# Gated attention mix: scaled V copies on VectorE, gate logits in one bank, paced loads, a last round in halves, and another order of semaphore waits

## The chip, the cores and the metric

One core of one Trainium2 chip. The time is the device time of one execution in microseconds (us), the median of several executions; the profile is of one of them, and its span is about 2 us shorter than the time. The engines are PE (TensorE matmuls; PEld is its weight loads), ACT (ScalarE), DVE (VectorE), POOL (GpSimd) and SP (the engine that issues most DMAs). The granted clock is the TensorE clock that the throttle allowed, as a share of full speed.

## The reference

```python
x = A_x                                          # (1, 2048, 512), bf16
g = sigmoid((x * gate_w).sum(-1, keepdims=True))
# A: softmax attention, 32 heads of 16
a = softmax(q @ k.T * 16 ** -0.5) @ v @ wo_A      # per head, 2048 x 2048 scores
# B: linear attention with phi(t) = where(t > 0, t + 1, exp(t)) + 1e-6
b = (phi(q) @ (phi(k).T @ v)) / (phi(q) @ phi(k).sum()) @ wo_B
out = g * a + (1 - g) * b
```

The time goes into A: 32 x 2048 x 2048 scores must be exponentiated. The kernel cuts them into rounds, each of 64 units of 128 x 512 scores.

## The kernel before

A scheduler written in Python walks through a model of the machine, decides the order of instructions on each engine, and then issues that order with semaphore waits. ACT does most of the exponentials, two units per instruction:

```python
return C(AC, 500, 427 * n + 49, lambda: nc.scalar.activation(
    P[:, slot, 0:512 * n], bank(b0, n), ACT.Exp, scale=ESC), ...)
```

The other units are evicted by VectorE as integers Z (a bit-pattern exponential), and shifted copies of Z, by VectorE or GpSimd, give further terms. Each term is multiplied on PE with a differently scaled copy of V. That is why V is scaled after its own eviction, here on GpSimd:

```python
for k in range(1, NTERM):
    yield po(690, lambda k=k: nc.gpsimd.tensor_scalar(Vc[:, k, vs]..., Vc[:, 0, vs]..., COEF[k], 1.0,
                                                      op0=ALU.mult, op1=ALU.mult), [r_V[vs]], [r_V[vs]])
```

An instruction names the semaphores that it must wait for in the order in which its operands are listed. Each becomes a wait ahead of the instruction:

```python
def add(self, fn, deps=(), inc=True, dma_sem=None):
    waits = []
    for d in deps:
        ...                                     # sem, val of the dependency
        for k, (s2, v2) in enumerate(waits):
            if s2 is sem:
                if val > v2:
                    waits[k] = (sem, val)
                break
        else:
            waits.append((sem, val))
...
for waits, fn, inc, dma_sem in E.ops:
    for sem, val in waits:
        eng.wait_ge(sem, val)
    h = fn()
```

The gate logits are computed in four PSUM banks, one per 512 rows of x, and everything behind them is engine work: a VectorE transpose per bank, a GpSimd copy, one exponential on ACT, a reciprocal, four reordering copies on VectorE. The weights of B (and those of A's later head groups) are loaded with one DMA each of 1.5 MB:

```python
def t_wb():
    yield ("DMA", wB[:], B_wqkv.rearrange("(cc p) n -> p cc n", p=128), semWB, 16, 12000.0, [], [r_wB], False, True)
```

The softmax here doesn't subtract the row's maximum and nothing guards it: scores larger than these inputs give would overflow.

## Time and profile before

| | before |
|---|---|
| time, median of 3 (range) | 681.13 (680.4 to 681.41) us |
| span of the profiled run | 679.8 us |
| first exponential starts | 10.67 us |
| exponentials of two units | 695, steady step 0.917 us |
| ACT time lost between first and last | 8.03 us: 6.61 up to 40 us, 0.11 from 40 to 80, 1.31 later |
| last exponential ends, tail behind it | 671.53, 8.30 us |

"ACT time lost" is worked out from the trace. For each pair of neighbouring ACT instructions between the first and the last exponential I take the step from end to end and subtract the undisturbed step: 0.917 us for an exponential of two units, 0.478 for one of the linear attention, 0.25 for the gate's.

Two views of before, to be held against the kernel after. The first is the chain of work that ended last, by engine; the second is what PE's weight loads waited for (us in total, times, longest):

```profile
ACT 42%; PE 42%; issue 14%; DVE 1%; DMA 1%; ACTq 0%; POOL 0%; POOLq 0%
```

```profile
PEld ps L363 <- ACT P L756: 239.9, 601, 0.8
PEld ps L363 <- issue: 116.0, 492, 0.8
...
PEld ps L363 <- DVE Z L672: 13.0, 52, 0.4
```

In the names, ps are the PSUM banks, Qz and KT what the score matmuls read, P ACT's exponentials, Z VectorE's, Vc the scaled copies of V. PE waits for ACT 601 times: the score matmuls of the next units may start only when an exponential has freed its banks. ACT sets the pace and PE follows it.

### The profile page before, as it was taken

How to read it: one execution, taken by the hardware profiler on the slowest of the kernel's cores; microseconds unless marked ns; L12 is line 12 of the kernel's file. 1: busy time of each engine (PE TensorE's matmuls, PEld its weight loads, DVE VectorE, ACT ScalarE, POOL GpSimd, SP SyncE). 2: the span in 40 equal slices, each digit the busy share in tenths (PEclk: the TensorE clock that was granted, in tenths of full speed). 3: DMA queues.
4: the chain of work that ended last, by engine and by line, in shares of the span. 5: the costliest groups of instructions: out<-in, count | busy, mean ns of one | idle time of the engine just before them, and what ended most of it. 6: DMA issues, size and time to landing. Idle time of an engine off the chain costs nothing.

```text
span 679.8 us, 24140 instructions
## 1 busy us (share of the span) xinstructions
PE 664.7 (98%) x9886; PEld 203.6 (30%) x9910; DVE 605.1 (89%) x1073; ACT 658.2 (97%) x734; POOL 550.7 (81%) x626
## 2 busy tenths in 40 slices
PE   8899999999999999999999999999999999999997
PEld 3323232322222222322333322222233322222222
DVE  5789889989899998989899998898999998998995
ACT  5799999999999999999999999999999999999995
POOL 4669878898888888888878888878589888889883
PEclk9999999999999999999999999999999999999999
DMA  6500002100000000000000100000003220000000
GB/s 132 203 18 3 9 2 72 33 2 10 2 9 2 7 6 2 10 2 2 12 3 23 52 10 1 10 3 2 1 11 53 38 49 25 17 18 17 18 18 32
DMA packets 27869, 15.96 MB, mean 23 GB/s; under 512 B 19697, under 2 KB 26737, under 8 KB 27761
## 3 DMA queue, kind: packets, MB, share of 16 engines
q1 hardware_dynamic: 26416, 13.91, 8.0%
q8 instruction: 79, 1.29, 0.8%
q10 hardware_dynamic: 1344, 0.52, 0.3%
q14 instruction: 30, 0.24, 0.1%
HBM read 6.69 MB, written 2.10 MB: 13 GB/s over the span
## 4 chain that ended last, share of the span: by engine, by line
ACT 42%; PE 42%; issue 14%; DVE 1%; DMA 1%; ACTq 0%; POOL 0%; POOLq 0%
ACT P L756 41%; PE ps L363 32%; PE ps L369 9%; ACT eb L1029 1%; DMA xnat<-wA 1%; DVE Z L672 0%; PE ps L884 0%; ACTq L1433 0%; DVE wA L1135 0%; DVE Z L734 0%; DVE T L994 0%; ACT KT L906 0%; ACT wA L1174 0%; POOL warm L407 0%; ACT gt L980 0%
## 5 line engine op out<-in xcount | busy, mean ns | idle before, releaser
L756 ACT ACTIVATE P<-ps 128x1024 bf16<-128x1024 f32 x695 | 645.3, 1126 | 7.4 <-PE ps L363 7.4
L724 POOL TENSOR_TENSOR Z<-Z,mcon 128x512 int32<-128x512 int32 x464 | 477.7, 1054 | 77.6 <-DVE Z L672 46.1
L672 DVE TENSOR_SCALAR Z<-ps 128x512 int16<-128x512 f32 x658 | 441.9, 683 | 57.0 <-PE ps L363 49.8
L363 PE MATMUL ps<-Z,Vc 128*17 128x512 bf16 x1974 | 283.8, 383 | 0.2
L363 PE MATMUL ps<-Qz,KT 32*128 32x512 bf16 x2048 | 272.1, 385 | 4.0 <-ACT P L756 2.3
L363 PE MATMUL ps<-P,Vc 128*17 128x512 bf16 x1390 | 253.0, 383 | 0.0
L363 PEld LDWEIGHTS ps<-Qz,KT 32*128 32x128 bf16 x2048 | 67.9, 91 | 260.4 <-ACT P L756 237.8
L363 PEld LDWEIGHTS ps<-Z,Vc 128*17 128x17 bf16 x1974 | 64.4, 88 | 78.2 <-issue 50.7
L734 DVE TENSOR_SCALAR Z<-Z 128x1024 int16<-128x1024 int16 x194 | 79.8, 430 | 0.2
L363 PEld LDWEIGHTS ps<-P,Vc 128*17 128x17 bf16 x1390 | 57.5, 88 | 55.1 <-issue 42.9
L363 PE MATMUL ps<-warm 128*32 128x512 bf16 (+13 forms) x618 | 59.3, 330 | 4.5 <-issue 3.0
L369 PE MATMUL ps<-xT,wA 128*32 128x512 bf16 x512 | 42.9, 382 | 0.0
L1030 POOL TENSOR_SCALAR eb<-eb 128x512 f32<-128x512 f32 x32 | 19.9, 622 | 16.9 <-DVE Z L734 7.4
L961 POOL TENSOR_SCALAR Vc<-Vc 128x576 bf16<-128x576 bf16 x32 | 21.9, 685 | 8.0 <-DVE Vc L958 5.2
L1017 POOL TENSOR_TENSOR T<-T,rg 128x256 bf16<-128x256 f32 x31 | 19.6, 634 | 8.6 <-DVE Z L734 5.3
L363 PEld LDWEIGHTS ps<-warm 128*32 128x32 bf16 (+1 forms) x642 | 20.8, 95 | 17.5 <-issue 10.3
L994 DVE STREAM_TRANSPOSE T<-ps 128x512 f32<-128x512 f32 x32 | 22.7, 709 | 3.0 <-PE ps L363 2.9
L369 PE MATMUL ps<-wA,xT 128*32 128x128 bf16 x1024 | 22.1, 220 | 2.2 <-issue 2.2
L369 PE MATMUL ps<-wB,xT 128*32 128x512 bf16 x256 | 23.4, 382 | 0.0
L369 PE MATMUL ps<-wA,OAT 128*32 128x512 bf16 x256 | 23.0, 381 | 0.0
L369 PE MATMUL ps<-xT,wB 128*32 128x512 bf16 x256 | 22.4, 383 | 0.0
L369 PE MATMUL ps<-wA,xnat 128*32 128x512 bf16 x256 | 22.3, 381 | 0.0
(79 smaller groups left out, 283.4 us busy)
## 6 DMA issues: line engine op xcount, KB each, us to landing
Qz<-QT SPq DMA_DIRECT2D x120, 16.0 KB, 1.8
wA<-in_A_wqkv_dram SPq DMA_DIRECT2D x1, 1536.0 KB, 7.8
wB<-in_B_wqkv_dram SPq DMA_DIRECT2D x1, 1536.0 KB, 11.9
xnat<-in_A_x_dram SPq DMA_DIRECT2D x3, 512.0 KB, 5.3
out_dram<-outt SPq DMA_DIRECT2D x12, 128.0 KB, 1.7
wA<-in_A_wo_dram SPq DMA_DIRECT2D x1, 512.0 KB, 4.3
wA<-in_B_wo_dram SPq DMA_DIRECT2D x1, 512.0 KB, 5.2
out_dram<-wA SPq DMA_DIRECT2D x4, 128.0 KB, 1.8
```

The source lines that it names most:

```text
L363: return lambda: nc.tensor.matmul(o, lhsT=l, rhs=r, start=start, stop=stop, skip_group_check=sg)
L369: h = nc.tensor.matmul(o[32 * j:32 * j + 32], lhsT=l[:, 32 * j:32 * j + 32], rhs=r, start=start, stop=stop, skip_group_check=True)
L672: return C(DV, 400, 533 * n + 74, lambda: nc.vector.tensor_scalar(o, i, ZB, 0.0, op0=ALU.add, op1=ALU.max), [r_bank[b] for b in bks], r_Z[ ...
L724: return C(PO, 400, 70 + 484 * n, lambda: nc.gpsimd.tensor_tensor(Z[:, z, 0:512 * n].bitcast(I32), Z[:, z0, 0:512 * n].bitcast(I32), mcon[ ...
L734: return C(DV, 450 if hot else 300, 69 + 134 * n, lambda: nc.vector.tensor_scalar(Z[:, z, 0:512 * n], Z[:, z0, 0:512 * n], float(m), None, ...
L756: return C(AC, 500, 427 * n + 49, lambda: nc.scalar.activation(P[:, slot, 0:512 * n], bank(b0, n), ACT.Exp, scale=ESC), [r_bank[b0 + k] fo ...
L961: yield po(690, lambda k=k: nc.gpsimd.tensor_scalar(Vc[:, k, vs].rearrange("p a b c -> p (a b c)"), Vc[:, 0, vs].rearrange("p a b c -> p ( ...
L994: yield dv(607, lambda: nc.vector.transpose(T1[:, a, :], bank(7)), [r_bank[7]], [r_T1[a]])
L1017: yield po(640, lambda: nc.gpsimd.tensor_tensor(t2[:, :, 16 * par:16 * par + 16], t1[:, :, 0:16], rg[:, a, :].unsqueeze(2).to_broadcast([1 ...
L1029: yield ac(480, lambda: nc.scalar.activation(eb[:, i, :], bank(b), ACT.Exp), [r_bank[b]], [r_eb[i]])
L1030: yield po(640, lambda: nc.gpsimd.tensor_scalar(eb[:, i, :], eb[:, i, :], 1.0 + 1e-6, 0.0, op0=ALU.min, op1=ALU.max), [r_eb[i]], [r_eb[i]])
```

## The change

It was meant to relieve GpSimd (the V copies go to VectorE), to shorten the gate's chain (one bank, 16 columns instead of 64 for the exponential, small SBUF-to-SBUF DMAs in place of transposes and copies), to stop large loads from holding all DMA engines (pieces of 384 KB, released over time), to start sooner (the first K only to half), to shorten the end (the last round in halves), and to let an instruction name last the semaphore that is expected last. Some constants of the scheduler were tuned again with it, so the order of instructions differs all over.

```diff
@@ waits of an instruction
-        for d in deps:
-            if d is None:
-                continue
+        for d in sorted([d for d in deps if d is not None], key=lambda d: d.fin if isinstance(d, _Ev) else 0.0):
...
                 if s2 is sem:
-                    if val > v2:
-                        waits[k] = (sem, val)
+                    val = max(val, v2)
+                    del waits[k]
                     break
-            else:
-                waits.append((sem, val))
+            waits.append((sem, val))
@@ scaled copies of V
-                yield po(690, lambda k=k: nc.gpsimd.tensor_scalar(Vc[:, k, vs]..., Vc[:, 0, vs]..., COEF[k], 1.0,
-                                                                  op0=ALU.mult, op1=ALU.mult), [r_V[vs]], [r_V[vs]])
+                yield ("OP", DV, 214, lambda k=k: nc.vector.tensor_scalar(Vc[:, k, vs]..., Vc[:, 0, vs]..., COEF[k], None,
+                                                                  op0=ALU.mult), [r_V[vs]], [r_V[vs]], None, 1.0, True)
@@ gate (both cut)
-            for qc in range(NQC):
-                b = yield ("BANK",)
-                ... matmuls with 128 columns, dv transpose of the bank, po copy to ge ...
-            yield ac(300, ... gt <- exp(-ge) ...)
-            ... po + 1, dv reciprocal, po 1 - g, four dv copies to gnat ...
+            b = yield ("BANK",)
+            ... matmuls of all four chunks, 32 rows each, one dv transpose ...
+            yield ac(230, ... ge[:, 0, :] <- exp(-gl) ...)
+            ... po + 1, dv reciprocal ...
             for qc in range(NQC):
+                for a in range(4):
+                    yield ("DMA", gt[32 * a:32 * (a + 1), qc, :], ge[32 * qc:32 * (qc + 1), 0, :], semGN, 256, 2500.0, ...)
+            ... po 1 - g, four DMAs to gnat ...
@@ loads
-        add_task(t_wb(), 0.9, 1, "WB")
+        for cc in range(NCC):
+            add_task(t_load(cc, NCC, wA[:, cc, :], wsrc[:, cc, :], semWA, 3500.0, ..., "wa"), 0.3 + 0.15 * cc, 0.9, f"WA{cc}")
+            add_task(t_load(cc, NCC, wB[:, cc, :], wsrcB[:, cc, :], semWB, 3500.0, ..., "wb"), 0.9 + 0.2 * cc, 1.8, f"WB{cc}")
@@ not shown: first K in halves, pairs of rounds sharing one reciprocal, last round in halves, 18 Z buffers for 16, scheduler constants
```

## The prediction

> **What bounds the kernel now.** I read the page's busy table first, then ACT's timeline over the whole span, then the groups, then the stages in windows.
>
> ```profile
> PE 664.7 (98%) x9886; PEld 203.6 (30%) x9910; DVE 605.1 (89%) x1073; ACT 658.2 (97%) x734; POOL 550.7 (81%) x626
> ...
> L756 ACT ACTIVATE P<-ps 128x1024 bf16<-128x1024 f32 x695 | 645.3, 1126 | 7.4 <-PE ps L363 7.4
> L724 POOL TENSOR_TENSOR Z<-Z,mcon 128x512 int32<-128x512 int32 x464 | 477.7, 1054 | 77.6 <-DVE Z L672 46.1
> L672 DVE TENSOR_SCALAR Z<-ps 128x512 int16<-128x512 f32 x658 | 441.9, 683 | 57.0 <-PE ps L363 49.8
> ...
> L734 DVE TENSOR_SCALAR Z<-Z 128x1024 int16<-128x1024 int16 x194 | 79.8, 430 | 0.2
> ...
> L961 POOL TENSOR_SCALAR Vc<-Vc 128x576 bf16<-128x576 bf16 x32 | 21.9, 685 | 8.0 <-DVE Vc L958 5.2
> ```
>
> PE shows 98% and ACT 97%. PE's share contains warm-up matmuls on a dummy tile that the program puts into free slots, so it cannot name the bound. ACT has no filler: 695 exponentials of two score units each. The other 658 units (695 x 2 + 658 = 2048) are done by VectorE and GpSimd with integer additions. In the 700-odd ACT instructions only 7.4 us of waiting stand before an exponential. From the records' ends I worked out the step from one exponential to the next: 651 of 660 neighbours are within 10 ns of 0.92 us. The longest unbroken run gives 0.917 (158.86 us for 173, less 0.2 us by which the last outlasts its step). So ACT is saturated from 36 us to 671 us, and the time is: start of the first exponential + 695 x 0.917 + 32 other exponentials of about 0.48 us each (start to the next start in the timeline) + ACT's idle + the tail behind the last exponential.
>
> Where ACT is not busy is in its timeline:
>
> ```profile
> 9.58 0.59 ACT L906 CAST KT<-ps 128x512 bf16<-128x512 f32 x1 [1.86 <-PE ps L369]
> 10.67 9.27 ACT L756 ACTIVATE P<-ps 128x1024 bf16<-128x1024 f32 x10 [0.50 <-PE ps L363]
> 21.18 8.36 ACT L756 ACTIVATE P<-ps 128x1024 bf16<-128x1024 f32 x9 [1.24 <-PE ps L363]
> 32.74 1.02 ACT L756 ACTIVATE P<-ps 128x1024 bf16<-128x1024 f32 x1 [3.21 <-PE ps L363]
> 35.62 28.52 ACT L756 ACTIVATE P<-ps 128x1024 bf16<-128x1024 f32 x31 [1.85 <-PE ps L363]
> ...
> 542.17 129.36 ACT L756 ACTIVATE P<-ps 128x1024 bf16<-128x1024 f32 x141 [0.36 <-PE ps L363]
> 675.67 1.23 ACT L1174 CAST wA<-ps 128x512 bf16<-128x512 f32 x2 [4.15 <-PE ps L369]
> ```
>
> The first exponential starts at 10.67 us. Then 1.24 us are lost at 20 us and 3.21 + 1.85 = 5.06 us around 30 to 36 us; later only 0.19 + 0.36. The last exponential ends at 671.53, 8.3 us before the span's end. The 5.06 us have their cause in these windows and in PE's timeline:
>
> ```profile
> 26.00:28.00 2.00, 2.00 (x60) 0.85 (x48) 2.00 (x4) 2.00 (x3) 1.92 (x3) 1.00 1.03 416
> 28.00:30.00 2.00, 0.71 (x30) 0.45 (x29) 0.83 (x2) 1.53 (x2) 1.28 (x2) 1.00 0.58 219
> 30.00:32.00 2.00, 1.11 (x10) 0.33 (x13) 0.77 (x2) 0.00 (x0) 0.00 (x0) 0.70 0.03 12
> 32.00:34.00 2.00, 2.00 (x23) 0.42 (x19) 0.97 (x3) 1.02 (x1) 1.83 (x3) 0.50 0.04 8
> ...
> 30.89 0.30 PE L369 MATMUL ps<-wA,xT 128*32 128x128 bf16 x4 [2.18 <-issue]
> ...
> wB<-in_B_wqkv_dram SPq DMA_DIRECT2D x1, 1536.0 KB, 11.9
> ```
>
> (Columns: stretch, length, busy PE, PEld, DVE, ACT, POOL, granted clock, DMA share, GB/s.) Two loads of 1.5 MB, issued at 19 and 19.5 us, hold all DMA engines from 22 to 29 us. At 28.7 us PE stops for 2.18 us in the middle of a group of equal matmuls, waiting for no engine ("issue"). The page counts 1.29 MB on an instruction queue of the same engines, and its packets of 16 KB come at 21.1 and only again at 28.5 us, just behind the loads. I read the gap as PE out of instructions. Afterwards the granted clock is 0.50 from 31 to 34 us, which stretches the loss.
>
> **What the Trainium skill says.** "Perfetto Trace Analysis", section Identifying the Most-Contended Engine: occupancy names the bound for Scalar and Vector, matmul busy time does not for Tensor. The trace agrees: PE's 98% contains fillers. "ScalarE: Activation LUTs", section What ACT_TABLE_LOAD costs: an ACTIVATE with a pointer bias takes about 280 ns + 0.833 per element, neighbours overlapping by about 93 ns. For 1024 columns that is 1133; the trace has 1126, but a step of 917, an overlap of 0.21 us; I use the measured step. "Runtime: NRT & Kernel Launch", section Instruction fetch mechanics: instructions come in blocks of 16 KiB over a DMA queue of the sequencer's own, mostly hidden. The trace shows such packets, and one that does not look hidden. "SBUF — State Buffer", section Who interferes with whom: a VectorE instruction in a two-port mode and a GpSimd instruction exclude each other. The scaled copies of V, moved to VectorE, would be such instructions; the program orders them against GpSimd with semaphores, as it does the 194 integer shifts.
>
> **The change part by part**, with counts from the order of instructions in the two programs.
>
> *Exponentials.* 693 instead of 695: 2 x 0.917 = -1.8 us. The gate's exponential shrinks from 128x64 (0.41 us) to 128x16: about -0.2.
>
> *V copies.* 32 of 0.685 leave GpSimd (-21.9 us); 32 come to VectorE. The 1024-column shift takes 0.43 and costs 79.8/194 = 0.41 of throughput; for 576 columns I estimate 0.26, so +8.3 us. Nine more shifts (+3.9) and four more evictions of scores (+2.7) come; pairing the reciprocals, four gate transposes fewer and no gate reordering on VectorE take away about 6.5. VectorE ends near 613, GpSimd near 520. Neither is on the path while ACT is saturated, so directly this is worth nothing.
>
> *The 1.24 us at 20 us.* Ten exponentials have run then and there are ten P buffers; the eleventh starts 0.45 us after the first P x V matmuls (20.73), which come behind V's scaled copies (GpSimd, 17.70 to 19.23). With copies of about 0.26 on VectorE the first P x V wave stands before one more score group than before, and starts with six P matmuls where it had two. I take -0.9 and leave 0.3.
>
> *Paced loads.* Each 1.5 MB load becomes four of 384 KB, released over about half a round, a round being about 20 us (655/32). At 416 GB/s a piece takes an estimated 0.95 us; between pieces instruction packets can pass. The 5.06 us go, I leave 0.3: -4.8.
>
> *K in halves.* Ahead of the first scores stand 16 matmuls of 256 columns in place of 16 of 512: the 32 before took 1.9 us, so 16 take 0.95 and halves save 0.45. The cast of K on ACT falls from 0.59 to about 0.37. Together -0.65 for the first exponential.
>
> *Last round in halves.* Before, from 672.53 to 674.95 one chain of five VectorE instructions (0.72, 0.26, 0.18, 0.43, 0.71), then casts to 676.91 and four output issues whose last lands at 679.34. Halves of about 0.40, 0.22, 0.17, 0.28, 0.40 with gaps of 0.03 make 1.6 us each: the first is done 0.8 us earlier, the second 0.8 later. The first two output tiles go out early, three of four casts on ACT, but the last issue still begins near 677.4 against 677.52 and takes the same 1.8 to land. So -0.2, not a microsecond.
>
> *Waits.* The reordered semaphore waits change when PE's sequencer gets to a matmul by fractions of 0.1 us; with ACT saturated and two score sets in turn, 0 on the path.
>
> Sum: -1.8 - 0.2 - 0.9 - 4.8 - 0.65 - 0.2 = -8.55, from 681.1: **672.5 us**, a ratio of 0.987.
>
> **The rivals.** (1) The gap at 30 us is not hunger for instructions but something that pacing does not move. For: one gap, once, and the packet landed (28.48 + 1.08) 1.3 us before PE went on. Against: it follows the only stretch with DMA share 1.0, on matmuls that wait for nothing. Then only about 3.8 us are gained: 677. (2) VectorE becomes the bound: the added 8 us plus port exclusion raise it from 89% to 91%, and score evictions come late, so the eviction banks stay full and PE delays score groups. For: the V copies cluster in the first rounds, where VectorE is already near 2.00 of 2.00 in some windows. Against: over the middle it has 5 to 10% free, and the offloaded units went up by four, not down. It would show as ACT idle of some microseconds at each V group: 676 to 680. (3) The saved GpSimd time lets the scheduler move more off ACT than counted. Against: the count is fixed, 693. (4) The tail gains more than I give, if the late casts overlap better: 671.5. (5) Smaller loads come too late for the second head group and idle ACT near 35 us: 674 to 676.
>
> **Range and chances.** The saturated middle is fixed by a count and a step and moves little; the head holds most of the uncertainty, more of it upwards. 8 in 10: 669 to 676.5. Faster by over 2% needs under 667.5, that is 5 us beyond a sum that already takes nearly all idle of the head: 0.07. Slower needs 694.8: 0.02. Within 2%: 0.91.
>
> **What would show it.** First exponential near 10.0; ACT idle between first and last exponential of about 1.2 us instead of 6.9; no PE "issue" gap over 1 us and a granted clock of 1.0 throughout 20 to 40 us; DMA share below 1.0 there; the step unchanged at 0.917 with 693 instructions; GpSimd busy near 520 and VectorE near 613; last exponential to end still about 8 us. I am wrong if ACT's step or its idle in the middle changed, if a gap remains at 30 us, or if the tail falls under 7 us.

## The result and the profile after

| | before | after |
|---|---|---|
| median (range) | 680.88 (680.4 to 681.41), 4 runs | 684.38 (683.45 to 685.51), 4 runs |
| span of the profiled run | 679.8 | 682.5 |
| first exponential | 10.67 | 9.88 |
| exponentials | 695 | 693 |
| ACT lost: up to 40, 40 to 80, later | 6.61, 0.11, 1.31 | 3.19, 4.29, 5.82 |
| tail | 8.30 | 8.31 |

The ratio is 1.0052, 95% interval 1.0035 to 1.0069. A ratio here is the mean time of one kernel's runs over the mean of the other's runs of the same rounds, so it is not quite the ratio of the medians. The kernel became slower by 3.5 us where 8.6 us less were predicted; 684.38 lies well outside the range of 669 to 676.5. All outputs are right.

The page of the kernel after: busy time by engine, the chain that ended last, and the group of exponentials:

```profile
PE 663.6 (97%) x9840; PEld 208.5 (31%) x9871; DVE 611.8 (90%) x1102; ACT 661.5 (97%) x733; POOL 517.9 (76%) x569
...
PE 85%; ACT 7%; issue 2%; DVE 2%; SPq 2%; POOL 1%; DMA 0%; ACTq 0%; DVEq 0%; POOLq 0%
...
L779 ACT ACTIVATE P<-ps 128x1024 bf16<-128x1024 f32 x693 | 646.0, 1046 | 8.0 <-PE ps L377 7.3
```

The busy row looks as predicted: VectorE 611.8 (613), GpSimd 517.9 (520), 693 exponentials. ACT still shows 97% and nearly the same idle as before (8.0 against 7.4). But the chain has gone from ACT to PE (which proves little: it is PE 72%, ACT 18% in e1 below, which is faster than before), and the mean record of an exponential has become shorter, 1046 ns instead of 1126, while the kernel became slower. In before, the record of an exponential starts 0.21 us before the earlier one ends (the median), in after only 0.115. After a real stop of ACT a record takes 1.024 us in both. So an exponential that is released a little later has a shorter record, and no gap is seen. The steps from end to end tell the truth: of some 660 steps, 651 are within 10 ns of 0.92 us in before and 577 in after. In after 82 are longer, 69 of them by no more than 0.16 us; in before it is 10.

What PE's weight loads waited for:

```profile
PEld ps L377 <- issue: 185.2, 679, 0.5
PEld ps L377 <- ACT P L779: 87.3, 226, 0.6
PEld ps L377 <- DVE Z L693: 45.4, 129, 0.8
PEld ps L377 <- DVE Z L757: 36.5, 95, 0.6
```

The waits for ACT fell from 239.9 to 87.3 us, while "issue" rose from 116.0 to 185.2 and those for VectorE from 13.0 to 45.4. VectorE's evictions didn't become slower (682 ns each, 683 before), and the idle time before the score matmuls' weight loads hardly moved: 260.4 us in before, 262.7 in after. What changed is mostly the semaphore that the weight load itself holds, and the profile puts a wait down to that. So these lines show what was reordered, but not yet that it costs anything.

ACT's timeline of the first 63 us (start, duration, instruction; in brackets the idle before it) and two stretches of the windows (columns: stretch, length, busy PE, PEld, DVE, ACT, POOL, granted clock, DMA share, GB/s):

```profile
9.88 9.32 ACT L779 ACTIVATE P<-ps 128x1024 bf16<-128x1024 f32 x10 [0.59 <-PE ps L377]
...
25.18 7.44 ACT L779 ACTIVATE P<-ps 128x1024 bf16<-128x1024 f32 x8 [1.36 <-PE ps L377]
...
35.17 15.85 ACT L779 ACTIVATE P<-ps 128x1024 bf16<-128x1024 f32 x17 [0.33 <-PE ps L377]
53.79 2.12 ACT L779 ACTIVATE P<-ps 128x1024 bf16<-128x1024 f32 x2 [2.77 <-PE ps L377]
56.81 5.81 ACT L779 ACTIVATE P<-ps 128x1024 bf16<-128x1024 f32 x6 [0.91 <-PE ps L377]
```

```profile
20.00:40.00 20.00, 19.79 (x404) 7.59 (x402) 18.97 (x39) 17.81 (x21) 11.69 (x13) 1.00 0.40 124
40.00:60.00 20.00, 16.84 (x247) 5.16 (x240) 14.60 (x26) 16.25 (x19) 12.16 (x13) 0.91 0.18 54
```

The 5.06 us around 30 to 36 us are gone, with a granted clock of 1.00 there, as predicted. In their place stand 2.77 + 0.91 us at 51 to 57 us, which before had not (ACT was busy for all of 40 to 60), and a clock of 0.91. What PE waited for there is in the timelines of SP's queue and of PE:

```profile
35.14 1.87 SPq L358 DMA_DIRECT2D Qz<-QT  x3
37.06 10.66 SPq L358 DMA_DIRECT2D gt<-ge  x16
47.76 4.06 SPq L358 DMA_DIRECT2D Qz<-QT  x5
```

```profile
53.29 0.39 PE L377 MATMUL ps<-Qz,KT 32*128 32x512 bf16 x3 [3.00 <-DMA Qz<-QT]
```

Sixteen copies of the gate, 0.67 us of SP's time each, stand between the third and the fourth of eight small DMAs that bring Q into place for the next rounds. PE has to wait 3.00 us for the last of these.

So there are three differences: 3.4 us gained in the head (5.7 predicted), 4.2 us lost at 51 to 57 us, and 4.5 us lost in small pieces all the way from 80 us to the end. With 0.8 us from the earlier start and 2.0 from the shorter list of exponentials and the gate's shorter one, they give -3.4 + 4.2 + 4.5 - 0.8 - 2.0 = +2.5, against +2.7 by the spans.

### The profile page after: what moved, and what is told of

It is laid out like the page before. It is cut to its first block, busy times and chain, and to the rows that moved or that the text cites. A ratio compares the mean times of both kernels' runs of the same rounds, so it can differ in the third digit from the quotient of the medians.

```text
span 682.5 us, 24083 instructions
## 1 busy us (share of the span) xinstructions
PE 663.6 (97%) x9840; PEld 208.5 (31%) x9871; DVE 611.8 (90%) x1102; ACT 661.5 (97%) x733; POOL 517.9 (76%) x569
## 3 DMA queue, kind: packets, MB, share of 16 engines
q8 instruction: 79, 1.29, 0.7%
## 4 chain that ended last, share of the span: by engine, by line
PE 85%; ACT 7%; issue 2%; DVE 2%; SPq 2%; POOL 1%; DMA 0%; ACTq 0%; DVEq 0%; POOLq 0%
PE ps L377 66%; PE ps L383 18%; ACT P L779 6%; SPq L358 2%; DVE Z L693 1%; POOL Z L747 1%; ACT eb L1090 1%; DVE Z L757 0%; DMA Qz<-QT 0%; PE ps L907 0%; DVE T L1042 0%; PE ps L1009 0%; DVE Qz L959 0%; DVE outt L1238 0%; DVE KT L942 0%
## 5 line engine op out<-in xcount | busy, mean ns | idle before, releaser
L779 ACT ACTIVATE P<-ps 128x1024 bf16<-128x1024 f32 x693 | 646.0, 1046 | 8.0 <-PE ps L377 7.3
L747 POOL TENSOR_TENSOR Z<-Z,mcon 128x512 int32<-128x512 int32 x459 | 470.0, 1047 | 118.7 <-PE ps L377 58.0
L377 PE MATMUL ps<-Z,Vc 128*17 128x512 bf16 x1986 | 280.9, 383 | 0.7 <-DVE T L1042 0.6
L377 PEld LDWEIGHTS ps<-Qz,KT 32*128 32x128 bf16 x2048 | 71.6, 91 | 262.7 <-ACT P L779 84.9
L757 DVE TENSOR_SCALAR Z<-Z 128x1024 int16<-128x1024 int16 x203 | 82.6, 421 | 0.2
L377 PE MATMUL ps<-warm 128*32 128x512 bf16 (+15 forms) x596 | 60.2, 321 | 5.2 <-issue 3.7
L383 PE MATMUL ps<-xT,wA 128*32 128x512 bf16 (+1 forms) x528 | 43.1, 376 | 0.1
L383 PE MATMUL ps<-phiK,xnat 128*32 128x512 bf16 x256 | 22.6, 382 | 0.0
L383 PE MATMUL ps<-wB,xT 128*32 128x512 bf16 x256 | 21.8, 382 | 0.0
L1092 DVE SCALAR_TENSOR_TENSOR phiK<-ps,eb 128x512 bf16<-128x512 f32 x32 | 21.7, 677 | 0.0
```

The source lines that it names most:

```text
L377: return lambda: nc.tensor.matmul(o, lhsT=l, rhs=r, start=start, stop=stop, skip_group_check=sg)
L383: h = nc.tensor.matmul(o[32 * j:32 * j + 32], lhsT=l[:, 32 * j:32 * j + 32], rhs=r, start=start, stop=stop, skip_group_check=True)
L747: return C(PO, 400, 70 + 484 * n, lambda: nc.gpsimd.tensor_tensor(Z[:, z, 0:512 * n].bitcast(I32), Z[:, z0, 0:512 * n].bitcast(I32), mcon[ ...
L757: return C(DV, 450 if hot else 300, 69 + 134 * n, lambda: nc.vector.tensor_scalar(Z[:, z, 0:512 * n], Z[:, z0, 0:512 * n], float(m), None, ...
L1092: yield dv(607, lambda: nc.vector.scalar_tensor_tensor(dst_ap, bank(b), 1e-6, eb[:, i, :], op0=ALU.max, op1=ALU.add), [r_bank[b], r_eb[i]] ...
```

## The experiments

Theories at this point. For the loss in small pieces ("the drip" in the expectations): the new order of waits makes PE late at each score group; rivals: the load added to VectorE, or the retuned constants with their other order of instructions. For the gap at 51 us: the gate's DMAs ahead of Q's in SP's queue; rival: the Q loads would have come too late anyway. For the head: pacing works as predicted; rival: it moves the gap.

First, what was issued. The programs were compared at a score matmul that waits for an exponential (its banks) and for VectorE. In shape:

```
before:  EventSemaphore  waits s_dve          after:  EventSemaphore  waits s_act
         Matmult         waits s_act                  Matmult         waits s_dve
```

An instruction holds one of its waits itself; the others stand ahead of it in a separate instruction. Here it is the wait that was named **first** that the matmul (in the trace, its weight load) holds: the list of before names ACT and then VectorE, that of after VectorE and then ACT. Of the score matmuls of before, 482 have VectorE's wait ahead and hold ACT's, and 186 have ACT's alone. In after, 408 have ACT's wait ahead and hold VectorE's, 67 are the other way round, and 188 have ACT's alone. So "last expected wait placed last" put the expected wait where it blocks the queue.

The sort turned round the waits of the other engines too, and those of ACT are on the same loop. In the trace of before, 693 of the 695 exponentials hold the wait for PE, and one for ACT's own earlier work stands ahead. In after, 683 of 693 hold ACT's own and have the wait for PE ahead.

Across all runs, with the loss of ACT by stretch of the profiled execution:

| run | median (range), us | ratio to before, 95% interval | first exp. | ACT lost: to 40, 40 to 80, later | exps, tail |
|---|---|---|---|---|---|
| before | 680.88 (680.4 to 681.41) | | 10.67 | 6.61, 0.11, 1.31 | 695, 8.30 |
| after | 684.38 (683.45 to 685.51) | 1.0052 [1.0035, 1.0069] | 9.88 | 3.19, 4.29, 5.82 | 693, 8.31 |
| e1_oldwaits | 678.76 (678.15 to 679.65) | 0.9976 [0.9959, 0.9992] | 9.71 | 2.73, 4.43, 1.82 | 693, 8.20 |
| e2_qzfirst | 684.76 | 1.0054 [1.0033, 1.0074] | 9.44 | 3.19, 5.73, 5.77 | 693, 8.29 |
| e3_old_qz | 680.18 | 0.9992 [0.9972, 1.0013] | 8.97 | 3.55, 5.40, 1.94 | 693, 8.20 |
| e4_newwaits | 686.17 | 1.0085 [1.0061, 1.011] | 10.95 | 6.70, 0.37, 5.84 | 695, 8.30 |
| e5_oldgate | 684.41 | 1.0063 [1.0048, 1.0078] | 8.83 | 6.37, 0.98, 2.46 | 696, 10.43 |
| e6_paced | 677.66 | 0.9963 [0.9947, 0.9979] | 10.68 | 3.11, 0.24, 1.29 | 695, 8.30 |
| e7_vdve | 684.64 | 1.0077 [1.0058, 1.0095] | 9.79 | 7.55, 0.77, 1.28 | 697, 10.73 |
| e8_oldconst | 679.45 | 0.9989 [0.9967, 1.0012] | 9.18 | 5.90, 0.22, 1.26 | 695, 8.35 |
| e9_gatedve | 675.59 (675.09 to 676.88) | 0.9928 [0.9911, 0.9945] | 10.14 | 3.03, 0.18, 1.16 | 693, 8.22 |
| e10_rev | 679.7 | 0.9979 [0.9958, 1.0001] | 9.17 | 3.60, 5.92, 0.83 | 693, 8.20 |
| e11_gatedve_rev | 675.21 (674.92 to 675.48) | 0.992 [0.9902, 0.9937] | 8.78 | 3.92, 0.02, 1.58 | 693, 8.22 |
| e12_paced_rev | 677.34 | 0.9951 [0.9935, 0.9968] | 9.56 | 4.10, 0.10, 0.33 | 695, 8.23 |

Before was run again beside each group (medians 680.53 to 681.08). The start of the first exponential differs by over 1 us between kernels that are the same up to there (8.97 in e3, 10.14 in e9), so one span does not tell a difference of 1 us; the stretches behind it and the medians do.

The fast state has two levels of its own. Of the 33 executions of before beside the experiments, 24 with a mean granted clock of 0.996 or 0.997 took 680.2 to 681.95 us, and nine at 1.0 took 677.89 to 679.8. The profiled one, at 0.997, has the clock at 0.50 from 30.8 to 34.2 us. So a difference of some 2 us between two kernels is to be read at one level. All executions of e9 and e11 and nearly all of e6 are at 1.0; those of after are at 0.995 to 0.998, those of e1 at 0.997 but for one.

### The order of waits: e1, e4, e10

**e1_oldwaits** is after with the old order of waits and nothing else; the order of instructions on each engine stays.

```diff
-        for d in sorted([d for d in deps if d is not None], key=lambda d: d.fin if isinstance(d, _Ev) else 0.0):
+        for d in deps:
+            if d is None:
+                continue
...
-                    val = max(val, v2)
-                    del waits[k]
+                    if val > v2:
+                        waits[k] = (sem, val)
                     break
-            waits.append((sem, val))
+            else:
+                waits.append((sem, val))
```

> The changed kernel with the waits in the order of the kernel before, the schedule of every engine unchanged. Theory W (placing the wait that is expected last at the end puts the ACT wait of a score matmul ahead and costs some 50 ns after each exponential's end, which uses up ACT's slack): the steps between exponentials go back to 0.92 us nearly everywhere, the drip of 5.8 us outside the two head gaps falls under 1.5 us, time 684.4 - 4.5 = about 680. Rival T (the new tuning constants load PE more than they assume, the order of waits is innocent): no change, 683.5 to 685.

**e4_newwaits** is the other half: before with the new order of waits alone.

```diff
+                ev.fin = fin                    # the modelled end, kept with each event
...
-        for d in deps:
-            if d is None:
-                continue
+        for d in sorted([d for d in deps if d is not None], key=lambda d: d.fin if isinstance(d, _Ev) else 0.0):
...                                              # and the append at the end, as in the change
```

> The kernel before with only the new order of waits. Theory W: the drip appears here too, +4 to +6 us, about 686; the S matmul starts about 50 ns later after the exponential's end than in the kernel before. Rival T: no change, 680.5 to 681.5.

e1 took 678.76, that is 5.6 us less than after, and its loss behind 80 us fell from 5.82 to 1.82 (4.0 us; its profiled execution, at 679.65, is the slowest of its six). e4 took 686.17 against 680.98 of before beside it, 5.2 us more, and its loss behind 80 us rose from 1.31 to 5.84, nearly the same figure as in after, though its schedule is that of before. Its waits and its exponentials look like those of after:

```profile
L755 ACT ACTIVATE P<-ps 128x1024 bf16<-128x1024 f32 x695 | 646.9, 1046 | 8.4 <-PE ps L362 7.2
```

And e1's waits of the weight loads look like those of before, with VectorE's added load still in place:

```profile
PEld ps L380 <- ACT P L782: 238.6, 596, 0.8
PEld ps L380 <- issue: 117.1, 504, 0.4
PEld ps L380 <- DVE Z L696: 14.6, 58, 0.4
```

So neither VectorE's load nor the schedule makes the small losses; the order of waits does, in both directions. The size of one: from the end of the latest exponential to the start of a score group's weight load, the lowest tenth is 51 ns in before, where the load holds ACT's wait, and 114 ns in after and 113 ns in e4 for loads with ACT's wait ahead. That is 63 ns later, by this measure, for some 400 of the 660 score groups. ACT answers later as well. An exponential before which ACT stood idle for over 20 ns starts 22 to 24 ns after PE's semaphore rose in before, e1 and e10 (all 33 of them), but 82 to 88 ns after it in after (16 of 18) and in e4 (11 of 21).

So the loop between ACT and PE became some 60 ns longer at both ends. e1, e4 and e10 change the waits of all engines together, so which end cost how much of the 5 us, and whether VectorE's or GpSimd's waits have a share, is not shown.

The Trainium skill fits this: by "Perfetto Trace Analysis", sections Sequencer-only Instruction and Tensor Engine Instruction, a wait of a sequencer-only instruction blocks the sequencer, which fetches the next instruction only when it is through, whereas a matmul is pushed into a hardware wait queue with its own wait and is already decoded when the semaphore comes. The trace agrees with the direction and gives the number for the weight load, 63 ns; that this is the time for fetching and decoding is the page's account and not shown by a run.

**e10_rev** turns the sort round, so that the wait expected last is named first (a second wait for the same semaphore now keeps its place, which is not shown).

```diff
-        for d in sorted([d for d in deps if d is not None], key=lambda d: d.fin if isinstance(d, _Ev) else 0.0):
+        for d in sorted([d for d in deps if d is not None], key=lambda d: -d.fin if isinstance(d, _Ev) else 0.0):
```

> The changed kernel with the new sorting of waits turned round: the wait that is expected last is named first. In the issued program the wait named first is carried by the matmul's weight load and the others stand ahead of it as a separate wait. Theory W2 (what is named last is not what is waited for last on the instruction, so the change did the opposite of its intent): as good as the old order, 678 to 679.5. Rival (any sorting by the model's expectation is worse than the old order): over 682.

679.7: 4.7 us less than after, and its loss behind 80 us is 0.83, the lowest of the kernels with this schedule, but the total is no better than e1's 678.76, because the loss from 40 to 80 us was 5.92 in this run and not 4.43. The windows show the clock with it (columns as above; two lines of e10, then the same two of e1):

```profile
56.00:58.00 2.00, 2.00 (x43) 0.93 (x35) 1.30 (x3) 1.09 (x2) 1.04 (x1) 0.50 0.13 35
58.00:60.00 2.00, 2.00 (x22) 0.40 (x22) 1.03 (x2) 1.63 (x2) 0.00 (x0) 0.56 0.07 17
```

```profile
56.00:58.00 2.00, 2.00 (x21) 0.40 (x18) 1.52 (x3) 1.86 (x2) 0.00 (x0) 0.63 0.10 25
58.00:60.00 2.00, 2.00 (x23) 0.54 (x24) 1.61 (x4) 1.96 (x3) 0.94 (x1) 1.00 0.08 18
```

The clock stood at 0.50 for 6.8 us in e10 and for 3.4 in e1. Four executions of e10 at a mean clock of 0.995 took 679.62 to 680.84, the two at 1.0 took 677.3 and 677.6, and the only one of e1 at 1.0 took 678.15. So the median of e10 is set by the clock. In the median, reversing the sort gives what the old order gave: the old order named ACT first at nearly all of these matmuls already.

### The gate's DMAs: e2, e3, e5, e9

**e2_qzfirst** and **e3_old_qz** move the five Q loads ahead of the sixteen gate copies in SP's queue, in after and in e1. The gate's values are then later by these five.

```diff
+        g0 = [k for k, o in enumerate(SP.ops) if o[3] is semGN]
+        q0 = [...]                              # the five Q loads that follow
+        SP.ops[g0[0]:g0[-1] + 1 + len(q0)] = q0 + SP.ops[g0[0]:g0[-1] + 1]
```

> The changed kernel with only five loads of Qz moved ahead of the sixteen small gate copies in the DMA queue of SP; all other engines as they are. Theory Q (the 16 gate copies of 0.67 us each keep Qz from landing and stop PE for 3 us at 50 us, then the clock falls): the gap at 50 to 57 us goes, -3.5 us, about 681. Rival (something else late there too, such as the gate itself): the gap moves to a later place and the time stays within 1 us of 684.4.

> Both together. If W and Q are separate causes they add: about 676.5, ACT idle between first and last exponential about 3 to 4.5 us. If they overlap (slack regained in one place is used up in the other), 678 to 681.

No gain: 684.76 against 684.38, and 680.18 against 678.76. The gap did not go, it moved to the other side of the swap. (The clock stood at 0.50 for 6.8 us in e2 and e3, against 3.4 in after and e1. At a mean clock of 0.997 e3 took 678.33 to 679.56 and e1 678.58 to 679.65, so at one level they are equal.) In e2, waits up to 66 us, and ACT's timeline:

```profile
POOL gp L1025 <- DMA gt<-ge: 4.4, 1, 4.4
...
PEld ps L377 <- POOL Z L747: 4.2, 2, 3.8
```

```profile
56.71 2.10 ACT L779 ACTIVATE P<-ps 128x1024 bf16<-128x1024 f32 x2 [4.29 <-PE ps L377]
```

GpSimd works in order. Its step behind the gate copies (1 - g) waited 4.4 us for them, the shifts of Z behind it came late, and PE waited 3.8 us for one of these. This shows that it isn't the place of Q's loads alone: the sixteen DMAs take 10.66 us of a queue, and both what stands behind them and what needs them is due within that time. The experiment failed to remove the cost but told what it is.

**e5_oldgate** is e1 with the whole gate of before.

> The changed kernel with the old order of waits and the gate of the kernel before (four banks, no copies by DMA). Theory G (the sixteen gate copies of 0.67 us each in SP's queue are too slow for any in-order engine behind them: with Qz behind them PE waits, with Qz ahead GpSimd waits for the gate and PE for it): the gap of 4 to 5 us between 40 and 60 us goes, about 674.5 against 678.8 with the old waits alone. Rival (a gap there in any case, such as the release of K, V and Q of the second head group): lost time of 40 to 80 us stays above 3 us, 678 to 680.

```diff
-            for h in range(2):
-                yield pe_step(2, 512, [g4(2 * h), g4(2 * h + 1)], ...)      # four chunks in one bank
-            ... sixteen DMAs to gt ...
+            for qc in range(NQC):
+                b = yield ("BANK",)
+                ... as in before: matmuls, transpose, copy; then exp, reciprocal, reordering copies on VectorE ...
```

684.41, and inconclusive for the total: the scheduler made another program of it (696 exponentials, a tail of 10.43, 6.37 us lost in the head). Only one stretch answers the question: from 40 to 80 us it lost 0.98 instead of 4.43. What was needed was a kernel in which nothing else moves.

**e9_gatedve** is that: e1 with the sixteen DMAs taken out of SP's finished list and seven small copies put into VectorE's finished list right behind the reciprocal. No instruction of any engine changes its place otherwise.

```diff
+        del SP.ops[g0[0]:g0[-1] + 1]                       # the sixteen DMAs
+        cps = [(w0 if qc == 0 else [], lambda qc=qc: nc.vector.tensor_copy(gt[0:32, qc, :], ge[32 * qc:32 * (qc + 1), 0, :]), False, semGN)
+               for qc in range(NQC)]
+        cps += [([(semGN, 64)] if a == 1 else [], lambda a=a: nc.vector.tensor_copy(gt[32 * a:32 * (a + 1), :, :], gt[0:32, :, :]), False, semGN)
+                for a in range(1, 4)]
+        DV.ops[at:at] = cps
```

> The changed kernel with the old waits; the sixteen gate copies by DMA are replaced by seven small VectorE copies behind the gate's reciprocal, every other instruction in its old place. Theory G: the gap of 4 us at 50 to 57 us goes with nothing else moved, lost ACT time of 40 to 80 us under 1 us, about 675 (e1 less 3.9, plus up to 0.5 for VectorE). Rival (the gap belongs to the second head group's loads or to VectorE): it stays, 678 to 679.

675.59, 3.2 us under e1 by the medians; the loss from 40 to 80 us fell from 4.43 to 0.18. ACT's timeline where the gap had been:

```profile
34.96 3.02 ACT L782 ACTIVATE P<-ps 128x1024 bf16<-128x1024 f32 x3 [0.32 <-PE ps L380]
38.17 20.43 ACT L782 ACTIVATE P<-ps 128x1024 bf16<-128x1024 f32 x22 [0.19 <-PE ps L380]
```

22 exponentials run without a stop from 38 to 58.6 us. So the gate's DMAs, and not a late Q as such, made the gap in this schedule. Six of e1's executions against six of e9's leave no overlap, and e1's one at a clock of 1.0 is still 2.6 us above e9's median.

### The loads, the V copies, the constants: e6, e7, e8

**e6_paced** is before with the paced loads alone.

```diff
-        dma(SP, wA[:], wsrc, semWA, 16, 9000.0, writes=[r_wA, r_wAk], issue=500.0)
-        add_task(t_wb(), 0.9, 1, "WB")
-        add_task(t_xn(), 5, 6, "XN")
+        for cc in range(NCC):
+            add_task(t_load(cc, NCC, wA[:, cc, :], ..., "wa"), 0.3 + 0.15 * cc, 0.9, f"WA{cc}")
+            add_task(t_load(cc, NCC, wB[:, cc, :], ..., "wb"), 0.9 + 0.2 * cc, 1.8, f"WB{cc}")
+        for g3 in range(3):
+            add_task(t_load(g3, 3, xnat[:, 4 + 4 * g3:8 + 4 * g3, :], ..., "xn"), 5 + 0.3 * g3, 6, f"XN{g3}")
```

> The kernel before with the paced loads alone. Theory L (the two loads of 1.5 MB starve PE of instructions): the issue gap of 2.18 us and the lowered clock go, ACT's lost time of the first 40 us falls from 6.6 to about 1.5 to 2, time about 676. Rival (pacing does not reach the gap): 680 to 682.

677.66, ratio 0.9963. It has the same 695 exponentials and the same tail, and its loss behind 80 us is 1.29 against 1.31, so the comparison is clean: the head's loss fell from 6.61 to 3.11. ACT's timeline:

```profile
21.19 8.36 ACT L758 ACTIVATE P<-ps 128x1024 bf16<-128x1024 f32 x9 [1.24 <-PE ps L366]
29.96 1.02 ACT L758 ACTIVATE P<-ps 128x1024 bf16<-128x1024 f32 x1 [0.42 <-PE ps L366]
32.13 28.52 ACT L758 ACTIVATE P<-ps 128x1024 bf16<-128x1024 f32 x31 [1.14 <-PE ps L366]
```

Of the 3.21 + 1.85 us that stood here before, 0.42 + 1.14 are left, and the 1.24 at 20 us are untouched. Pacing works but is worth 3.5 us in this trace, not 4.8: 1.56 us remain. By the medians it is 2.9 us (680.53 before). Part of it is the clock: the executions of before beside it that were at 1.0 took 677.89 to 679.46, those of e6 at 1.0 676.71 to 678.19, about 1 us less on the mean. So of some 3 us, by an estimate from three executions of before and five of e6, about 2 go with the clock at 0.50. That the stop of PE brings this clock about was not tested.

**e7_vdve** is before with the V copies on VectorE alone.

> The kernel before with the scaled copies of V on VectorE alone. My theory: off the path while ACT is saturated, within 1.5 us of 681. Rival V (VectorE becomes late, score evictions delayed, ACT idles): 683 to 687, with lost time spread over the stages in which V is made.

```diff
-                yield po(690, lambda k=k: nc.gpsimd.tensor_scalar(..., COEF[k], 1.0, op0=ALU.mult, op1=ALU.mult), ...)
+                yield ("OP", DV, 214, lambda k=k: nc.vector.tensor_scalar(..., COEF[k], None, op0=ALU.mult), ..., None, 1.0, True)
```

684.64, 4 us more, where within 1.5 us of 681 was expected. The copies' own cost isn't seen in it: with the constants of before the scheduler makes 697 exponentials of it (two more: 1.8 us) and a tail of 10.73 (2.4 more). The profiled execution, at 686.87 and a clock of 0.997, is the slowest of the six; the four at 1.0 took 684.36 to 684.71. The loss of ACT from 40 us on is 2.05, against 1.42 in before. So in steady state the copies cost little, and what they do in the head (7.55 lost against 6.61) can't be told from this run.

**e8_oldconst** is e1 with the scheduler's constants and priorities of before.

> The changed kernel with the old waits and the constants and priorities of the kernel before: only the structural parts remain. Theory: the constants are worth little; apart from the 4 us gap of the gate copies the middle is saturated as in the kernel before, 677 to 681 for its 697 or fewer exponentials. Rival (the new constants are what makes the changed schedule hold): over 683.

```diff
-    FILL = 0.725
+    FILL = 0.755
-    BACK = 980.186
-    SHB = 3
+    BACK = 1005.06
+    SHB = 2
... about twenty such values ...
```

679.45 against 678.76: the retuning is worth nothing that can be seen, and its loss from 80 us on is as low as everywhere with the old waits (1.26). Where the time went in it differs, though: 5.90 in the head and 0.22 at 40 to 80. It is another schedule with the same sum. It also bounds what e9 shows: the sixteen gate copies stand in SP's queue here too, ahead of five Q loads, and ACT runs through.

```profile
36.63 11.54 SPq L361 DMA_DIRECT2D gt<-ge  x16
...
34.59 28.67 ACT L782 ACTIVATE P<-ps 128x1024 bf16<-128x1024 f32 x31 [1.53 <-PE ps L380]
```

So the gap of 40 to 80 us comes from these DMAs together with after's constants; the schedule of e8 had lost 3.2 us more in the head than e1's and comes to these loads later. Whether that or its other order of instructions spares it was not separated.

### Together: e11, e12

**e11_gatedve_rev** joins the edits of e9 and e10, shown above: the change with both faults removed. **e12_paced_rev** joins those of e6 and e10 on before.

> e9 with the waits of e10: the changed kernel with its two costs mended and its intent kept. If both theories hold: 674 to 676, 0.8% under the kernel before and the best of the kernels tried.

> The kernel before with paced loads and the reversed order of waits. Since its old order already lets the weight load of a score matmul carry the ACT wait, nothing beyond the paced loads: 677 to 678.

e11 took 675.21 (674.92 to 675.48), ratio 0.992 to before and 9.2 us less than after. It is the best kernel, though within the interval of e9 (675.59). e12 took 677.34 against 677.66 of e6: on the schedule of before, reversing the waits gains nothing that can be told apart by the time (ratios 0.9951 and 0.9963, with overlapping intervals). Its loss behind 80 us is the lowest of all, 0.33 against 1.29, but in one trace each, and the head lost 1.0 more.

### The head, left open

In all kernels with after's schedule, 2.7 to 3.9 us remain lost up to 40 us, where I predicted 0.6. The timeline of e1 around its largest piece:

```profile
23.33 0.30 DVE L999 TENSOR_SCALAR Vc<-Vc 128x576 bf16<-128x576 bf16 x1
...
23.88 0.30 DVE L999 TENSOR_SCALAR Vc<-Vc 128x576 bf16<-128x576 bf16 x1
...
24.25 0.10 PEld L380 LDWEIGHTS ps<-P,Vc 128*17 128x17 bf16 x5 [0.28 <-DVE Vc L999]
...
24.70 1.02 ACT L782 ACTIVATE P<-ps 128x1024 bf16<-128x1024 f32 x1 [1.31 <-PE ps L380]
```

ACT stands still for 1.31 us until P x V matmuls have run, and these waited for the second scaled copy of V, which on VectorE had its place behind score evictions and an integer shift. The ten P buffers then hold back the next exponential. This is read from one timeline. An eleventh P buffer doesn't fit beside this kernel's 18 Z buffers, and giving up Z buffers for it would change the schedule again, so no clean run tests it, and I leave it open.

## Why the prediction was wrong

The predicted parts against the measured ones, in us of span, before to after:

| step of the prediction | predicted | measured |
|---|---|---|
| exponentials, 693 for 695, and the gate's | -2.0 | -2.0 (counts and step as predicted; the cost by the step) |
| K in halves, first exponential | -0.65 | -0.79 |
| gap at 20 us and paced loads (ACT lost up to 40 us) | -5.7 | -3.4 |
| gate copies (ACT lost from 40 to 80 us) | not in the sum | +4.2 |
| waits (ACT lost behind 80 us) | 0 | +4.5 |
| last round in halves (tail) | -0.2 | 0.0 |
| sum | -8.55 | +2.5 by parts, +2.7 by the spans |

**Waits: the step that failed most.** The prediction held that the reordering changes PE "by fractions of 0.1 us; with ACT saturated and two score sets in turn, 0 on the path". The fraction was right, 63 ns. The zero was wrong, and so was the unstated direction. ACT's saturation doesn't protect it: PE comes to each score group only as ACT frees its banks, so PE's reaction time lies in the loop between the two engines. ACT's own reaction lies in it too, and the prediction did not think of ACT's waits at all: these came some 60 ns later as well. The slack in it differs from group to group. Where it is used up, the next step of ACT becomes longer than 0.93 us, 82 times in after and 24 times in e1. Undone on all engines, 5.6 us came back; done alone on before, 5.2 us were lost. I had not looked at which of two named waits an instruction holds. The compiled program of before and after would have shown it without any run.

**The gate's DMAs: a cost left out.** The prediction counts the "four gate transposes fewer and no gate reordering on VectorE" as relief for VectorE and does not ask what replaces them. The cost was there to be counted: 16 issues on SP's in-order queue at about 0.67 us, 10.7 us in the middle of eight loads that PE needs. It is worth 3.2 us by the medians of e9 and e1, about 4.2 by the loss in the stretch, in the schedule that after's constants make.

**The head: right mechanism, too large a size.** The gap at 30 us was what pacing moves: e6 alone got 3.5 us, and in after the granted clock is 1.00 in 20 to 40 us and no matmul or weight load waits over 0.5 us for its issue. The first rival ("something that pacing does not move") is refuted. But I left 0.3 for it where 0.42 + 1.14 remained in e6. And the gap at 20 us, for which I took -0.9, was not removed but became several, with 1.36 at 24 us in after. The scaled copy took 0.301 us on VectorE, not 0.26, and, more than that, waited for VectorE's other work. And about 2 us of what pacing gained go with the clock at 0.50, which the faster executions of before don't seem to have either (see e6).

**What was right.** The step of 0.917 with 693 instructions where nothing waits, the first exponential at 9.88 (10.0 predicted), the busy times of VectorE (611.8, 613 predicted) and GpSimd (517.9, 520), and that halving the last round gives no whole microsecond. That the first exponential hit 10.0 so closely is in part luck: it starts at 9.56 to 10.95 in the kernels with the old start (e4, e6, e7, e12, before) and at 8.78 to 10.14 in those with K in halves. On the mean that is 10.33 against 9.34. No run shows the port exclusion that the prediction cites. The second rival, VectorE as the bound, didn't come about: e1 and e9 have the same VectorE load and lose 1.82 and 1.16 us behind 80 us. The test that the prediction set itself, "if ACT's step or its idle in the middle changed", is what went off.

With both faults out, e11 is at 675.21; the rest to 672.5 is about what the head loses.

## What to carry to other kernels

An instruction held one wait itself in these programs, and it was the one named first: name first the wait that comes last on the critical loop, on both of its engines, and look in the compiled program whether it sits on the instruction or ahead of it. Moving work from engines to small DMAs isn't free when one in-order queue issues them: count the issues, look what stands behind them, and when they must be complete. Before two kernels are compared to a microsecond or two, look at the granted clock of each execution. And when a saturated engine gets slower, compare steps from end to end: occupancy, idle and mean duration of its records can all look the same or better while it loses time.

## What the Trainium skill lacked or had wrong

- "Perfetto Trace Analysis", Identifying Dependency Chains: it says that further waits are put ahead in EventSemaphore instructions, not which wait stays with the instruction nor what the place costs. Here the first named stays; with the critical wait ahead, the score matmul's weight load started 114 ns after the exponential's end at the lowest tenth, against 51 ns, and an exponential 82 to 88 ns after PE's semaphore, against 22 to 24; together 5.2 to 5.6 us of some 680.
- "Perfetto Trace Analysis", Identifying the Most-Contended Engine: occupancy is named as a fair measure for Scalar. ACT had 661.5 us (97%) busy in after and 657.7 (97%) in e1, though after lost 4.3 us more to waiting: records of neighbours overlap, so that a later release only shortens the record (1046 ns on the mean, 1122 in e1).
- "ScalarE: Activation LUTs", What ACT_TABLE_LOAD costs: it says by how much neighbours overlap, about 93 ns, not that the records of a queue overlap by more. After a stop an exponential's record took 1.024 us here and the step is 0.917, so 107 ns fit the page; but in unbroken runs the records took 1126 ns on the mean in before, up to 1249, and overlapped by 209. So neither the mean record nor its overlap is a cost.
- "Runtime: NRT & Kernel Launch", Instruction fetch mechanics: "mostly hidden". PE stopped for 2.18 us with no engine to wait for behind two loads of 1.5 MB, and with the loads in pieces no weight load or matmul waited over 0.5 us in that way (e6 and after). That it was the instruction fetch is an inference from the packets of that queue, not proven by a run.
- "DMA: Bandwidth & Descriptors", Issuing engines are not separate DMA queues: the sequencer time for initiating a DMA is called usually small relative to the DMA itself. For copies of 2 KB it was 0.67 us each, against 1.7 us from issue to landing, and 10.66 us for sixteen; in the schedule of after it was this that cost 3 to 4 us.
